# A fused attention and two-layer MLP kernel: the second layer's weights, activations and partial sums handled by other engines, at other times

## The chip, the cores and the metric

One core of one Trainium2 chip runs the whole program. The metric is device microseconds (us) of one execution. Five engines work side by side: TensorE (PE; its weight loads are shown as PEld), VectorE (DVE), ScalarE (ACT), GpSimd (POOL) and SyncE (SP), which here only issues DMAs. Each engine takes its instructions strictly in the order in which they were recorded, so an instruction that waits holds up all that stand behind it on its engine.

## The reference

Inputs are q, k, v (2 batches, 8 heads, 768 tokens, 64 wide, float32) and four weight matrices in float64. An attention with a local window and 24 block summaries gives x (1536 tokens by 512), and two MLP layers follow:

```python
x = attention(q, k, v)                     # 1536 x 512
h = x @ moe_w_in                           # 512 -> 2048
x = (maximum(h, 0) + log1p(exp(-abs(h)))) @ moe_w_out
h = maximum(x @ moe2_w_in, 0)              # second layer
return (h * h) @ moe2_w_out                # 2048 -> 512, float32
```

## The kernel before

Every float32 matrix product is made of three products of rounded parts: each operand is split into a high part (hi, a rounded copy) and a low part (lo, operand minus hi), and TensorE adds hi by hi, hi by lo and lo by hi. So each operand costs a copy and a subtraction on another engine before TensorE may use it.

**First layer** (lines 669 to 730). Weights are held as 16 chunks of 128 hidden columns, in nine slots in SBUF. A step is one chunk by 512 tokens: 12 matmuls into one bank of PSUM (L680), softplus and the hi copy on ScalarE (L686, L687), the lo part on VectorE (L689), and, two steps later, 12 matmuls with the output weights (L706). At the end of a block of tokens the four output banks are added into `part` (L729, VectorE).

**Second layer** (`second`, L792 to L1087). It works in 16 *quads*; a quad is two hidden chunks (f) by one half of the tokens (z, 0 or 1). The first product of a quad is done by Winograd's form of Strassen's scheme, with seven half-size products in place of eight:

- *Activations* (`prepare`, L844 to L890). For each half z, four differences of blocks of `part` (`diff`, L877) and seven splits into hi (L869, ScalarE) and lo (L868, VectorE or GpSimd) give B11, B21, B22, T1 to T4. They are made once per half.
- *Weights* (`w_in`, `w_out`). The float64 words are loaded into one of the `raw` buffers and joined to float32 (`fetch`: L630 on ScalarE, L635 on VectorE, a rescaling copy, L635 again); four sums and differences S1 to S4 (`calc`, L913) and the hi and lo parts (L314/L316 and L927, L940) follow. Of the four raw buffers three (raw0 to raw2) rotate; raw3 holds partial sums.
- *Products* (`quad_in`). `product` is six matmuls of 384 columns (L984) into one of two banks, h0 and h1; here the text calls the seven of a quad p0 to p6. Before, each next product goes to the other bank, and sums of products that Winograd's scheme needs are made in SBUF: `add` (L991, VectorE) adds a bank to a tile `raw3`, `t0` or `t1`.
- *Gates* (`gate`). relu and square (L998), hi (ScalarE), lo (L1001), for each of the four quarters of the hidden block.
- *Outputs* (`quad_out`). Six groups of six matmuls (L1046), here o0 to o5, which work on the gates of the quad before; o0 and o1 go to the two banks of the tile `accp`. When the quads pass to the other half of the tokens, the six banks are first taken out (ACT copy the first time, later L1058 on VectorE: *evacuation*).

TensorE's order within a quad is p0 p1 o0 p2 o1 p3 o2 p4 o3 p5 o4 p6 o5.

**What sets the order.** All work is recorded through `op(engines, costs, due, fn, r, w)` and then laid out by a list scheduler (`Plan.run`, L95): each engine in turn takes, of what is ready by the costs, the operation with the earliest due time; where an operation names two engines, the one that would end first gets it. The due times of the second layer count from T0, the planned end of the first, and from QT per quad. The result is one fixed queue per engine. `rel` holds a load back to 110 us before its due time.

```python
801  quads = [(((q + 1) // 2) % N2, ((q + 2) // 2 + 1) % 2 if q % 2 else (q // 2) % 2) for q in range(2 * N2)]
892  prepare(0, T0 - 20.0)
893  prepare(1, T0 + 8.0)
965  U, V_, C21, E = 3 + q % 2, 0, 1, 2
968  return hb[(q + j) % 2][:, 0:384]
1077 w_in(u, Tq[uses[u][0]])
```

So the quads before are (f, z) = (0,0) (1,0) (1,1) (2,1) (2,0) (3,0) (3,1) ... (7,1) (7,0)... and (0,1) at the end, and each set of weights serves two quads that follow each other, but for the first and the last (nine sets).

Of the kernel before, what the change touches and what calls it, by code (L numbers as in the profile page):

```python
# [8 lines left out]
F32 = mybir.dt.float32  # L9
# [4 lines left out]
ALU = mybir.AluOpType  # L14
# [173 lines left out]
def kernel(  # L188
# [119 lines left out]
    def tt(e):  # L308
        return nc.gpsimd if e == "POOL" else nc.vector
# [304 lines left out]
    def fetch(i, which, wi, wo, f, dl, dv, due):  # L614
# [23 lines left out]
        op(("ACT", "DVE"), (0.75, 0.85), dv, three, w=[RL], rel=due - HOLD)  # L638
        op("DVE", 0.95, dv, lambda: join(ALU.bitwise_and, 0x80000000), r=[RH], w=[RL])
        op(("ACT", "POOL"), (0.67, 0.8), dv, lambda e: copy(e, hi.bitcast(F32), hi.bitcast(F32), 2.0 ** -112), w=[RH])  # L640
        op("DVE", 0.95, dv, lambda: join(ALU.logical_shift_left, 3), r=[RH], w=[RL])
# [150 lines left out]
    def second(T0):  # L792
# [8 lines left out]
        quads = [(((q + 1) // 2) % N2, ((q + 2) // 2 + 1) % 2 if q % 2 else (q // 2) % 2) for q in range(2 * N2)]  # L801
        uses = [[0]] + [[2 * u - 1, 2 * u] for u in range(1, N2)] + [[2 * N2 - 1]]
# [41 lines left out]
        def prepare(z, due):  # L844
# [7 lines left out]
            def split(n, at, due):  # L852
# [39 lines left out]
        prepare(0, T0 - 20.0)  # L892
        prepare(1, T0 + 8.0)
# [8 lines left out]
        def w_in(u, due):  # L902
# [3 lines left out]
            for i, c in ((i0, 2 * f), (i1, 2 * f + 1)):  # L906
                fetch(i, 0, w2_in, w2_out, c, due - 32.0, due - 6.0, due)
# [4 lines left out]
            def calc(to, x, y, o, r, w, d):  # L912
                op(("POOL", "DVE"), (0.8, 0.5), due - 5.0 + d, lambda e: tt(e).tensor_tensor(out=to, in0=x, in1=y, op=o), r=r, w=w)  # L913
# [6 lines left out]
            for j, (x, k_, n) in enumerate(((a, A0, 512), (s12, A1, 512), (s34, B1, 512), (b[:, R_], B0, 256))):  # L920
# [4 lines left out]
                op(("ACT", "POOL"), (0.2 + 0.47 * n / 512, 0.2 + 0.6 * n / 512), d, lambda e, o=o_, j=j, x=x: copy(e, o(j), x),  # L925
                   r=[k_, *key], w=[("wi", u % 2, j, "h")])
                op(("POOL", "DVE"), (0.2 + 1.2 * n / 512, 0.2 + 0.8 * n / 512), d, lambda e, o=o_, j=j, x=x: tt(e).tensor_tensor(  # L927
                    out=o(4 + j), in0=x, in1=o(j).bitcast(F32), op=ALU.subtract), r=[k_, ("wi", u % 2, j, "h"), *key], w=[("wi", u % 2, j, "l")])

        def w_out(v, due):  # L930
            f = quads[uses[v][0]][0]
            for u in range(2):
                i, s = next_raw(), W_OUT[v % 2]
                lo, hi = halves(i)
                fetch(i, 1, w2_in, w2_out, 2 * f + u, due - 32.0, due - 6.0, due)
                o_h, o_l = (ws[s][n] for n in (("ih", "il"), ("oh", "ol"))[u])
# [20 lines left out]
        ng = [0]  # L957
        gat = {}

        def quad_in(q):  # L960
# [33 lines left out]
            def gate(x, f_, blk):  # L994
                i = ng[0] % len(gp)
                ng[0] += 1
                gat[q, f_, blk] = i
                op("DVE", 0.56, URG, lambda: nc.vector.scalar_tensor_tensor(  # L998
                    out=tmp[x], in0=tmp[x], scalar=0.0, in1=tmp[x], op0=ALU.max, op1=ALU.mult), w=[kt(x)])
# [147 lines left out]
    for i, x in enumerate(pend):  # L1147
        finish(x, T + 1.5 + 2 * 2.9 * i, 2.9)
# [42 lines left out]
```

## Time and profile before

| | |
|---|---|
| three runs | 612.46, 613.47 (median), 615.49 us |
| the profiled execution | 614.31 us; span on the core 612.6 us |
| busy, share of the span | PE 590.9 us (96%), DVE 398.9 (65%), POOL 314.8 (51%), ACT 299.8 (49%) |
| granted TensorE clock, mean | 0.988 of full speed |
| chain that ended last, by engine | PE 75%, DVE 14%, DMA 5%, ACT 2% |

"Busy" counts the time from an instruction's start to its end, a wait for a port within it included. The chain is followed back from the last instruction to what released each step. In the lists of groups, "idle" is what an engine waited just before them. Matmuls overlap: six that are listed with 1.21 us follow each other within 1.04 us.

### The profile page before, as it was taken

The numbers are of one execution on the slowest core, as the hardware profiler recorded it, in microseconds if no ns is written. First come the engines' busy times: TensorE is split into PE (matmuls) and PEld (weight loads), VectorE is DVE, ScalarE is ACT, GpSimd is POOL, SyncE is SP. The second block draws the span as 40 slices with busy tenths as digits, with TensorE's granted clock in tenths as the row PEclk, the third lists the DMA queues.
The fourth block names the chain that finished last, engine by engine and source line by source line (L and its number), as shares of the span: only waits on it lengthen the run. The fifth ranks groups of instructions, "written<-read, shape, count | busy, mean of one in ns | idle before, by whom it ended". The sixth has DMA issues, their size and how long they took to land.

```text
span 612.6 us, 9978 instructions
## 1 busy us (share of the span) xinstructions
PE 590.9 (96%) x3905; PEld 517.3 (84%) x3905; DVE 398.9 (65%) x556; ACT 299.8 (49%) x531; POOL 314.8 (51%) x296
## 2 busy tenths in 40 slices
PE   9798999999999999999999997999999999999997
PEld 7677988999888888888888886898888898989996
DVE  5898999726564142652138799876586868687633
ACT  4686888856664144441136363745435343444220
POOL 5877796525650042540018586747565556556421
PEclk9799999999999999999999997999999999999999
DMA  9999622423541032220000420222222222221112
GB/s 283 247 289 224 164 65 56 117 70 109 169 135 35 0 94 80 70 69 1 0 1 1 137 68 1 69 70 70 68 70 68 70 71 69 70 68 35 56 49 103
DMA packets 65871, 53.46 MB, mean 87 GB/s; under 512 B 36384, under 2 KB 59936, under 8 KB 65824
## 3 DMA queue, kind: packets, MB, share of 16 engines
q1 hardware_dynamic: 65824, 52.83, 30.0%
q8 instruction: 30, 0.49, 0.4%
q14 instruction: 17, 0.14, 0.1%
HBM read 49.68 MB, written 3.15 MB: 86 GB/s over the span
## 4 chain that ended last, share of the span: by engine, by line
PE 75%; DVE 14%; DMA 5%; ACT 2%; issue 2%; SPq 1%; POOL 1%; DVEq 0%; ACTq 0%
PE h L680 17%; PE h L984 17%; PE accp L706 10%; PE acc L706 7%; PE acc L1046 7%; PE accp L1046 7%; PE h L1046 7%; DVE raw L635 3%; DMA late<-in_v_dram 2%; DMA raw<-in_moe_w_out_dram 2%; DVE part L877 1%; DVE sm L524 1%; DVE mx L538 1%; DVE s L507 1%; DVE x L868 1%
## 5 line engine op out<-in xcount | busy, mean ns | idle before, releaser
L635 DVE SCALAR_TENSOR_TENSOR raw<-raw 128x512 uint32<-128x512 uint32 x136 | 117.3, 876 | 36.6 <-ACT raw L630 26.7
L680 PE MATMUL h<-x,wih 128*128 128x512 f32 (+1 forms) x480 | 125.4, 349 | 0.0
L680 PEld LDWEIGHTS h<-x,wih 128*128 128x128 f32 x480 | 83.6, 189 | 11.9 <-issue 0.5
L680 PE MATMUL h<-x,wil 128*128 128x512 f32 (+1 forms) x240 | 83.3, 347 | 0.3 <-POOL wil L606 0.3
L686 ACT ACTIVATE h<-h 128x512 f32<-128x512 f32 (+1 forms) x60 | 29.9, 500 | 94.3 <-PE h L680 93.9
L630 ACT ACTIVATE raw<-raw 128x512 uint32<-128x512 uint16 x63 | 42.3, 675 | 39.4 <-DMA raw<-in_moe_w_out_dram 27.8
L680 PEld LDWEIGHTS h<-x,wil 128*128 128x128 f32 x240 | 45.4, 189 | 6.1 <-POOL wil L606 0.5
L984 PE MATMUL h<-x,wil 128*128 128x384 f32 x192 | 39.6, 341 | 2.5 <-ACT woh L314 2.5
L316 POOL TENSOR_SCALAR wih<-raw 128x512 fp32r<-128x512 f32 x17 | 11.6, 683 | 58.4 <-PE h L680 44.8
L314 ACT ACTIVATE raw<-raw 128x512 f32<-128x512 f32 x44 | 29.5, 674 | 21.3 <-DVE raw L635 21.1
L984 PE MATMUL h<-x,wih 128*128 128x384 f32 x192 | 39.3, 340 | 0.3 <-ACT raw L314 0.3
L984 PEld LDWEIGHTS h<-x,wil 128*128 128x128 f32 x192 | 34.8, 192 | 4.2 <-ACT woh L314 2.8
L984 PEld LDWEIGHTS h<-x,wih 128*128 128x128 f32 x192 | 35.0, 192 | 3.2 <-ACT raw L314 0.6
L868 POOL TENSOR_TENSOR x<-part,x 128x768 fp32r<-128x768 f32 x8 | 17.8, 2230 | 37.7 <-ACT x L314 37.7
L316 POOL TENSOR_SCALAR raw<-raw 128x512 f32<-128x512 f32 x24 | 18.2, 765 | 30.1 <-DVE raw L635 27.8
L689 DVE TENSOR_TENSOR g1l<-h,g1h 128x256 fp32r<-128x256 f32 (+1 forms) x24 | 13.2, 549 | 26.2 <-ACT g1h L687 26.2
L984 PE MATMUL h<-x,woh 128*128 128x384 f32 x144 | 29.1, 337 | 0.7 <-DVE t L991 0.7
L913 POOL TENSOR_TENSOR raw<-raw 128x256 f32<-128x256 f32 x25 | 22.6, 906 | 13.7 <-DVE raw L635 6.3
L544 POOL TENSOR_TENSOR s<-s,sm 128x960 f32<-128x960 f32 (+1 forms) x14 | 22.1, 1579 | 13.5 <-DVE sm L526 12.6
L984 PEld LDWEIGHTS h<-x,woh 128*128 128x128 f32 x144 | 25.7, 188 | 3.5 <-DVE t L991 1.5
L991 DVE TENSOR_TENSOR t<-raw,h 128x384 f32<-128x384 f32 x32 | 17.6, 551 | 14.7 <-PE h L984 13.7
L606 POOL TENSOR_TENSOR wol<-raw,woh 128x512 fp32r<-128x512 f32 x14 | 19.8, 1411 | 14.3 <-ACT woh L314 13.9
(349 smaller groups left out, 1588.9 us busy)
## 6 DMA issues: line engine op xcount, KB each, us to landing
raw<-in_moe_w_in_dram SPq DMA_DIRECT2D x34, 512.0 KB, 4.3
raw<-in_moe_w_out_dram SPq DMA_DIRECT2D x34, 512.0 KB, 3.4
vwin<-in_v_dram SPq DMA_DIRECT2D x20, 192.0 KB, 5.3
part<-in_k_dram SPq DMA_DIRECT2D x12, 256.0 KB, 5.0
late<-in_v_dram SPq DMA_DIRECT2D x2, 1536.0 KB, 10.8
out_dram<-part SPq DMA_DIRECT2D x12, 256.0 KB, 2.0
part<-in_q_dram SPq DMA_DIRECT2D x10, 256.0 KB, 5.2
vwin<-in_v_dram SPq DMA_DIRECT2D x4, 160.0 KB, 5.6
```

Of the source, the lines that this page charges most:

```text
L314: nc.scalar.activation(out=out_, in_=in_, func=AF.Copy, **({} if mul is None else {"scale": mul}))
L316: tt(e).tensor_scalar(out=out_, in0=in_, scalar1=1.0 if mul is None else mul, scalar2=1.0, op0=ALU.mult, op1=ALU.mult)
L544: op(("POOL", "DVE"), (1.8 * n + 0.1, 1.75 * n), due, lambda e, sv=sv, rv=rv, spread=spread: tt(e).tensor_tensor(out=sv, in0=sv, in1=sprea ...
L630: nc.scalar.activation(out=lo, in_=q4[:, :, 1], func=AF.Copy, scale=2.0 ** -13, bias=-4095.5 / 8192.0)
L635: nc.vector.scalar_tensor_tensor(out=lo, in0=hi, scalar=n, in1=lo, op0=how, op1=ALU.bitwise_or)
L680: nc.tensor.matmul(out=hview(st), lhsT=ws[s][wn][:, w_], rhs=xx[bl][:, kk, o:o + n], start=(kk == 0 and xx is xh and wn == "ih"), stop=(kk ...
L686: op("ACT", ta, due, lambda: nc.scalar.activation(out=hview(st), in_=hview(st), func=AF.Softplus), w=[H_], tab="sp")
L706: nc.tensor.matmul(out=o, lhsT=a[:, sl], rhs=b, start=(st["first"] and c == 0 and not (A and m % 2)), stop=(st["last"] and c == 2 and not ...
L868: tt(e).tensor_tensor(out=l, in0=i, in1=h.bitcast(F32), op=ALU.subtract)
L913: op(("POOL", "DVE"), (0.8, 0.5), due - 5.0 + d, lambda e: tt(e).tensor_tensor(out=to, in0=x, in1=y, op=o), r=r, w=w)
L984: nc.tensor.matmul(out=bk(b), lhsT=ws[i][m][:, c], rhs=half((z, x, xp), kk), start=first and kk == 0 and n == 0, stop=kk == 1 and n == 2, ...
L1046: nc.tensor.matmul(out=out_bank(j), lhsT=x[:, cs], rhs=y, start=first and u == 0 and n == 0, stop=last and u == 1 and n == 2)
```

## The change

It edits `second` and the little around it:

- **Order of quads:** (0,0) (1,0) (2,0) (2,1) (3,1) (3,0) (4,0) ... (6,1) (7,1) (7,0) (0,1) (1,1). The first three quads work on half 0, so half 1 is wanted at the fourth quad and no more at the third; the last two need chunk pairs 0 and 1 again, which makes ten sets of weights (two more loads of each matrix).
- **Due times:** the activations of half 0 are due at T0 - 27 (before: T0 - 20), of half 1 at T0 + 24 (before: T0 + 8); the first two sets of weights at T0 - 80 and T0 - 45 (w_in), T0 - 75 and T0 - 40 (w_out).
- **Products:** even steps of Winograd's sum stay in bank h0, and TensorE adds the next product onto them; ScalarE copies the sum out between (`keep`). h1 takes p1, p3, p6. Three `add` are left of five. The quarter C21 is squared straight from the bank.
- **Engines:** `diff`, the lo parts of the activations and of the gates go to VectorE alone; `calc` and the lo parts of the weights to GpSimd alone; their hi parts and the two conversions of `fetch` to ScalarE alone.
- The last steps of the first layer are given slightly more planned time (3.6 for 2.9).

```diff
-        quads = [(((q + 1) // 2) % N2, ((q + 2) // 2 + 1) % 2 if q % 2 else (q // 2) % 2) for q in range(2 * N2)]
-        uses = [[0]] + [[2 * u - 1, 2 * u] for u in range(1, N2)] + [[2 * N2 - 1]]
+        quads, uses = [(0, 0), (1, 0), (2, 0)], []
+        while len(quads) < 2 * N2 - 2:
+            f, z = quads[-1]
+            quads += [(f, 1 - z), (f + 1, 1 - z)] if f + 1 < N2 else [(f, 1 - z)]
+        quads += [(0, 1), (1, 1)]
...
-                op(("POOL", "DVE"), (2.0, 1.0), due, lo, r=[K[at], ("x2", z, n, "h")] + lk[z, n, "l"], w=[("x2", z, n, "l")])
+                op("DVE", 0.9, due, lambda: lo("DVE"), r=[K[at], ("x2", z, n, "h")] + lk[z, n, "l"], w=[("x2", z, n, "l")])
...
-        prepare(0, T0 - 20.0)
-        prepare(1, T0 + 8.0)
+        prepare(0, T0 - 27.0)
+        prepare(1, T0 + 24.0)
...
-                op(("POOL", "DVE"), (0.8, 0.5), due - 5.0 + d, lambda e: tt(e).tensor_tensor(out=to, in0=x, in1=y, op=o), r=r, w=w)
+                op("POOL", 0.85, due - 5.0 + d, lambda: nc.gpsimd.tensor_tensor(out=to, in0=x, in1=y, op=o), r=r, w=w)
...
-            U, V_, C21, E = 3 + q % 2, 0, 1, 2
+            U, V_, C21, U2 = 0, 1, 2, 3 + q % 2
 
             def bk(j):
-                return hb[(q + j) % 2][:, 0:384]
+                return hb[j][:, 0:384]
...
-                op(("POOL", "DVE"), (1.1, 0.56), URG, lambda e: tt(e).tensor_tensor(
+                op("DVE", 0.56, URG, lambda: nc.vector.tensor_tensor(
                     out=gview2(i)[1], in0=tmp[x], in1=gview2(i)[0].bitcast(F32), op=ALU.subtract),
...
+            def keep(x, b):
+                op("ACT", 0.5, URG, lambda: copy("ACT", tmp[x], bk(b)), r=[kb_(b), *r3], w=[kt(x)])
             product(0, "A11", "B11", 0, True)
-            op("ACT", 0.5, URG, lambda: copy("ACT", tmp[U], bk(0)), r=[kb_(0), *r3], w=[kt(U)])
-            product(1, "S2", "T2", 1, True)
+            keep(U, 0)
+            product(1, "A12", "B21", 1, True)
             add(U, U, 1)
-            product(2, "A12", "B21", 0, False)
-            op("ACT", 0.5, URG, lambda: nc.scalar.activation(out=tmp[E], in_=bk(0), func=AF.Relu), r=[kb_(0), *r3], w=[kt(E)])
-            gate(E, 0, 0)
-            product(3, "S3", "T3", 1, True)
-            add(V_, U, 1)
-            product(4, "S1", "T1", 0, True)
-            product(5, "A22", "T4", 1, False)
-            add(C21, U, 1)
-            gate(C21, 1, 0)
+            gate(U, 0, 0)
+            product(2, "S2", "T2", 0, False)
+            keep(U2, 0)
+            product(3, "S1", "T1", 1, True)
+            product(4, "S3", "T3", 0, False)
+            keep(V_, 0)
+            add(V_, V_, 1)
+            gate(V_, 1, 1)
+            product(5, "A22", "T4", 0, False)
             yield
-            add(V_, V_, 0)
-            gate(V_, 1, 1)
-            product(6, "S4", "B22", 0, False)
-            add(U, U, 0)
-            gate(U, 0, 1)
+            gate(C21, 1, 0, 0)
+            product(6, "S4", "B22", 1, False)
+            add(U2, U2, 1)
+            gate(U2, 0, 1)
...
-            w_in(u, Tq[uses[u][0]])
-            w_out(u, Tq[uses[u][0] + 1])
+            w_in(u, T0 - (80.0, 45.0)[u])
+            w_out(u, T0 - (75.0, 40.0)[u])
```

What it moves, at three places. In all of them raw_74 to raw_77 are raw0 to raw3, t_1818 and t_1819 are t0 and t1, h_107 and h_108 are h0 and h1, x tiles hold the split activations, and tiles named wih, wil, woh, wol with a number are parts of the weight slots.

*GpSimd's queue across the passage from the first layer to the second*, before:

```order
L868 TENSOR_TENSOR x_73<-part,x_73 128x768
L877 TENSOR_TENSOR part<-part 128x2x384 x2
L868 TENSOR_TENSOR x_73<-part,x_73 128x768 x2
L868 TENSOR_TENSOR x_1817<-part,x_1817 128x768
L316 TENSOR_SCALAR wil_87<-raw_75 128x512
L927 TENSOR_TENSOR wih_90<-raw_75,wih_86 128x512
L927 TENSOR_TENSOR woh_92<-raw_76,woh_88 128x512
L940 TENSOR_TENSOR wil_95<-raw_74,wih_94 128x512
```

and of the change:

```order
L935 TENSOR_TENSOR wih_90<-raw_75,wih_86 128x512
L935 TENSOR_TENSOR wil_91<-raw_75,wil_87 128x512
L935 TENSOR_TENSOR woh_92<-raw_76,woh_88 128x512
L935 TENSOR_TENSOR wol_93<-raw_76,wol_89 128x256
L948 TENSOR_TENSOR wil_95<-raw_74,wih_94 128x512
L948 TENSOR_TENSOR wol_97<-raw_75,woh_96 128x512
```

The four subtractions and two differences of activations are gone from this queue; all lo parts of the second set of weights stand on it, four of which VectorE shared before.

*VectorE's queue after the last evacuation of the middle block of the first layer* (L729 into `part`), of the change; L689 is the lo part of a first-layer step, L885 is `diff` and L876 the lo part of an activation:

```order
L729 TENSOR_TENSOR part<-acc_1821,part 128x512
L885 TENSOR_TENSOR part<-part 128x2x384 x2
L876 TENSOR_TENSOR x_1817<-part,x_1817 128x768
L876 TENSOR_TENSOR x_73<-part,x_73 128x768
L885 TENSOR_TENSOR part<-part 128x2x384
L876 TENSOR_TENSOR x_73<-part,x_73 128x768
L885 TENSOR_TENSOR part<-part 128x2x384
L876 TENSOR_TENSOR x_73<-part,x_73 128x768
L689 TENSOR_TENSOR g1l<-h_107,g1h 128x512
```

Before, one difference and one subtraction of half 0 stood ahead of that L689 on VectorE, one of each behind it, and the rest on GpSimd; now all eight stand between that L729 and the L689.

*ScalarE's queue in one quad of the steady stretch*, before (L1010 takes p2 out of its bank):

```order
L314 ACTIVATE raw_77<-h_107 128x384
L1010 ACTIVATE edge<-h_107 128x384
L314 ACTIVATE woh_1805<-edge 128x384
L630 ACTIVATE raw_74<-raw_74 128x512
L630 ACTIVATE raw_76<-raw_76 128x512
L314 ACTIVATE raw_76<-raw_76 128x512
L314 ACTIVATE g0h<-t_1818 128x384
```

and of the change, from the copy of p0 (t_1818<-h_107) to the one that frees h0 for p5 (t_1819<-h_107):

```order
L314 ACTIVATE t_1818<-h_107 128x384
L314 ACTIVATE woh_84<-raw_74 128x512
L314 ACTIVATE wih_86<-raw_75 128x512
L314 ACTIVATE woh_1805<-t_1818 128x384
L314 ACTIVATE raw_77<-h_107 128x384
L630 ACTIVATE raw_76<-raw_76 128x512
L314 ACTIVATE raw_76<-raw_76 128x512
L630 ACTIVATE raw_74<-raw_74 128x512
L314 ACTIVATE t_1819<-h_107 128x384
```

Where ScalarE read a bank twice early in a quad, it now reads one four times, and the third of these stands behind two conversions (L630) that wait for a DMA and a rescaling copy that waits for VectorE.

## Rows read from the trace of the kernel before

**Rows 1.** Busy time by stretch: the passage between the layers, the steady stretch; columns named.
```profile
core 0: us, PE busy (x) PEld busy (x) DVE busy (x) ACT busy (x) POOL busy (x), PEclk, DMA share, GB/s
343.00:386.00 43.00, 37.67 (x172) 32.74 (x171) 42.40 (x48) 22.32 (x42) 33.43 (x24) 0.92 0.16 49
395.54:600.72 205.18, 203.97 (x1015) 182.70 (x1015) 142.16 (x208) 81.18 (x147) 113.13 (x105) 1.00 0.19 62
```
**Rows 2.** Waits of PE, 319 to 381 us, then 381 to 601 us: total, times, longest.
```profile
PE h L984 <- ACT woh L314: 2.5, 1, 2.5
PE h L984 <- DVE t L991: 2.5, 2, 1.8
...
PE accp L1046 <- DVE part L1058: 1.2, 2, 0.6
```
**Rows 3.** Timeline of PE from the second layer's first product: start, duration, [idle before].
```profile
341.83 1.23 PE L984 MATMUL h<-x,wih 128*128 128x384 f32 x6
...
367.99 1.62 PE L984 MATMUL h<-x,wol 128*128 128x384 f32 x6 [1.77 <-DVE t L991]
369.41 0.63 PE L1046 MATMUL h<-wih,wih 128*128 128x512 f32 x1
369.83 0.63 PE L1046 MATMUL h<-wil,wih 128*128 128x512 f32 x1
...
379.18 2.26 PE L984 MATMUL h<-x,wil 128*128 128x384 f32 x6 [2.52 <-ACT woh L314]
```
**Rows 4.** The chain of waits: start, duration, what; the fourth and fifth quad, then the end.
```profile
395.54 2.08 PE h L984 x12
397.62 1.39 PE accp L1046 x6
...
411.18 2.08 PE h L984 x12
...
600.72 2.73 PE accp L1046 x12
```
**Rows 5.** Timeline of VectorE in the passage, then of GpSimd.
```profile
361.82 2.60 DVE L877 TENSOR_TENSOR part<-part 128x768 f32<-128x768 f32 x1
...
364.81 2.20 DVE L868 TENSOR_TENSOR wih<-part,woh 128x384 fp32r<-128x384 f32 x1
...
364.50 2.09 POOL L877 TENSOR_TENSOR part<-part 128x768 f32<-128x768 f32 x1 [0.90 <-DVE part L877]
```
**Rows 6.** Single lines, whole run: duration ns min/median/max, first and last start.
```profile
L991 DVE TENSOR_TENSOR raw<-raw,h x32: 536/542/555, 347.0 to 599.4; 128x384 f32<-128x384 f32 x32
...
L998 DVE SCALAR_TENSOR_TENSOR t<-t x32: 546/558/2165, 352.0 to 597.6; 128x384 f32<-128x384 f32 x32
...
L868 DVE TENSOR_TENSOR x<-part,x x4: 946/2036/2637, 309.2 to 369.8; 128x768 fp32r<-128x768 f32 x4
...
L635 DVE SCALAR_TENSOR_TENSOR raw<-raw x136: 642/694/2282, 13.0 to 566.7; 128x512 uint32<-128x512 uint32 x136
...
L1001 POOL TENSOR_TENSOR wol<-t,woh x10: 1010/1020/1452, 379.2 to 580.8; 128x384 fp32r<-128x384 f32 x10
...
L940 POOL TENSOR_TENSOR wil<-raw,wih x9: 1311/1331/1738, 260.4 to 570.1; 128x512 fp32r<-128x512 f32 x9
```
**Rows 7.** Timeline, one quad of the steady stretch: p2 on PE, its reader on ACT.
```profile
509.29 1.21 PE L984 MATMUL h<-x,wih 128*128 128x384 f32 x6
...
510.60 0.49 ACT L1010 ACTIVATE edge<-h 128x384 f32<-128x384 f32 x1 [2.85 <-PE h L984]
```
**Rows 8.** Timeline of ACT: second conversion of a quad, two late ones.
```profile
469.58 0.67 ACT L630 ACTIVATE raw<-raw 128x512 uint32<-128x512 uint16 x1 [0.25 <-DMA raw<-in_moe_w_in_dram]
...
514.49 0.68 ACT L630 ACTIVATE raw<-raw 128x512 uint32<-128x512 uint16 x1 [0.83 <-DMA raw<-in_moe_w_in_dram]
```
**Rows 9.** Timeline around o1 of a quad that evacuates: DVE, then PE.
```profile
478.20 0.68 DVE L1058 TENSOR_TENSOR part<-accp,part 128x512 f32<-128x512 f32 x1
...
478.93 0.50 PE L1046 MATMUL accp<-wih,woh 128*128 128x512 f32 x1 [0.63 <-DVE part L1058]
```

More of the change, by code (lines that the diff above doesn't have):

```diff
@@ L612, in halves, with fetch @@
         return r[:, :, 0], r[:, :, 1]
-    def fetch(i, which, wi, wo, f, dl, dv, due):
+    def fetch(i, which, wi, wo, f, dl, dv, due, own=False):
         lo, hi = halves(i)
@@ L637, in fetch @@
         op("SP", 0.6, dl, load, w=[RL, RH], kb=348, rel=due - HOLD - 10.0)
[L638 to L641, printed above, removed]
+        op(*(("ACT", 0.67) if own else (("ACT", "DVE"), (0.75, 0.85))), dv, (lambda: three("ACT")) if own else three, w=[RL], rel=due - HOLD)
+        op("DVE", 0.75 if own else 0.95, dv, lambda: join(ALU.bitwise_and, 0x80000000), r=[RH], w=[RL])
+        op(*(("ACT", 0.67) if own else (("ACT", "POOL"), (0.67, 0.8))), dv, lambda e="ACT": copy(e, hi.bitcast(F32), hi.bitcast(F32), 2.0 ** -112), w=[RH])
+        op("DVE", 0.75 if own else 0.95, dv, lambda: join(ALU.logical_shift_left, 3), r=[RH], w=[RL])
     g_t, tmp = [], []
@@ L800, in second @@
         N2 = NF // 2
-        quads = [(((q + 1) // 2) % N2, ((q + 2) // 2 + 1) % 2 if q % 2 else (q // 2) % 2) for q in range(2 * N2)]
-        uses = [[0]] + [[2 * u - 1, 2 * u] for u in range(1, N2)] + [[2 * N2 - 1]]
+        quads, uses = [(0, 0), (1, 0), (2, 0)], []
[3 more added lines that the diff above has]
+        quads += [(0, 1), (1, 1)]
+        for q, (f, z) in enumerate(quads):
+            if q and quads[q - 1][0] == f:
+                uses[-1].append(q)
+            else:
+                uses.append([q])
         use_of = {q: u for u, x in enumerate(uses) for q in x}
@@ L876, in flat @@
                     return v if S[n][0] == 3 or 3 not in bs else v.rearrange("p k (b t) -> p k b t", b=3)
-                op(("DVE", "POOL"), (1.0, 2.0), due, lambda e: tt(e).tensor_tensor(
+                op("DVE", 0.9, due, lambda: nc.vector.tensor_tensor(
                     out=flat(to), in0=flat(a), in1=flat(b_), op=ALU.subtract),
@@ L934, in w_out @@
                 lo, hi = halves(i)
-                fetch(i, 1, w2_in, w2_out, 2 * f + u, due - 32.0, due - 6.0, due)
+                fetch(i, 1, w2_in, w2_out, 2 * f + u, due - 32.0, due - 6.0, due, True)
                 o_h, o_l = (ws[s][n] for n in (("ih", "il"), ("oh", "ol"))[u])
                 k_ = ("raw", i, 0)
-                op(("ACT", "POOL"), (0.67, 0.8), due - 4.0, lambda e, o_h=o_h, lo=lo: copy(e, o_h, lo.bitcast(F32)),
+                op("ACT", 0.67, due - 4.0, lambda o_h=o_h, lo=lo: copy("ACT", o_h, lo.bitcast(F32)),
                    r=[k_, ("slot", s)], w=[("wo", v % 2, u, "h")])
-                op(("POOL", "DVE"), (1.4, 1.0), due - 4.0, lambda e, o_h=o_h, o_l=o_l, lo=lo: tt(e).tensor_tensor(
+                op("POOL", 1.4, due - 4.0, lambda o_h=o_h, o_l=o_l, lo=lo: nc.gpsimd.tensor_tensor(
                     out=o_l, in0=lo.bitcast(F32), in1=o_h.bitcast(F32), op=ALU.subtract),
@@ L956, in out_bank @@
             return acc[j] if j < 4 else hb[j - 2]
-        ng = [0]
+        gfree = list(range(len(gp)))
         gat = {}
@@ L992, in add, with gate, square @@
                    r=[kb_(b)] + ([kt(x)] if x != to else []), w=[kt(to)])
[L994 to L996 removed]
+            def gate(x, f_, blk, psum=None):
+                i = gfree.pop(0)
                 gat[q, f_, blk] = i
[L998 to L999 removed]
+                def square():
+                    if psum is None:
+                        nc.vector.scalar_tensor_tensor(out=tmp[x], in0=tmp[x], scalar=0.0, in1=tmp[x], op0=ALU.max, op1=ALU.mult)
+                    else:
+                        nc.vector.tensor_tensor(out=tmp[x], in0=bk(psum), in1=tmp[x], op=ALU.mult)
+                if psum is not None:
+                    op("ACT", 0.5, URG, lambda: nc.scalar.activation(out=tmp[x], in_=bk(psum), func=AF.Relu),
+                       r=[kb_(psum), *r3], w=[kt(x)])
+                op("DVE", 0.56, URG, square, r=[] if psum is None else [kb_(psum)], w=[kt(x)])
                 op("ACT", 0.52, URG, lambda: copy("ACT", gview2(i)[0], tmp[x]), r=[kt(x), gp[i]], w=[("gg", i, "h")])
[L1001 removed]
+                op("DVE", 0.56, URG, lambda: nc.vector.tensor_tensor(
                     out=gview2(i)[1], in0=tmp[x], in1=gview2(i)[0].bitcast(F32), op=ALU.subtract),
@@ L1061, in quad_out @@
                     op("SP", 0.5, due, lambda t=t, pt=pt: nc.sync.dma_start(out=out[128 * t:128 * t + 128, :], in_=pt), r=[kp], kb=256)
+            gfree.extend(gat[q, u, blk] for u in range(2) for blk in sorted({j // 3 for j in js}))
             if last and 5 in js:
@@ L1147 @@
     for i, x in enumerate(pend):
[L1148 removed]
+        finish(x, T + 2.0 + 2 * 3.6 * i, 3.6)
     second(T)
```

8 lines of the change are left out of this document (4 added, 4 removed).

## Prediction

> **What bounds the kernel now.** I read busy time by stretch first [rows 1]. In the steady stretch of the second layer, 395.54 to 600.72 us, PE is busy 203.97 of 205.18 us at full clock, and VectorE, ScalarE and GpSimd have 63, 124 and 92 us to spare. In the passage from the first layer to the second, 343 to 386 us, it is the other way round: PE 37.67 of 43 at a clock of 0.92, VectorE 42.40 of 43, GpSimd 33.43. So time can be won in the passage, and elsewhere there is little to win.
>
> How much? The chain [rows 4] gives the price of a quad: the fourth begins at 395.54, the fifth at 411.18, so 15.64 us, made of seven products of 1.04 (two in 2.08) and six output groups of 1.39. Thirteen quads fill 395.54 to 600.72: 13 x 15.64 = 203.3, so 1.9 us are lost there. From the first product at 341.83 [rows 3] to 395.54 there are 53.71 us. What PE has to do in it is three quads, without outputs for the first (6 x 1.39 = 8.34 less), and the last 24 matmuls of the first layer (four groups' worth, 5.56): 46.92 - 8.34 + 5.56 = 44.14. So 9.6 us are lost in the passage, **11.4 us in all**, and a change that leaves the matmuls alone can win no more.
>
> Where the 9.6 go: PE's waits [rows 2] hold a wait of 2.5 for a hi copy on ScalarE and 2.5 for two adds on VectorE, and a little more; the two long ones stand in PE's timeline at 367.99 and 379.18 [rows 3]. That is some 5.3 with short ones. The rest is the clock: behind the first of these waits matmuls of 512 columns start 0.42 apart (369.41, 369.83), against 1.39 / 6 = 0.23 in the steady stretch. The granted clock falls after PE has waited, to the lower of its levels, so each wait is paid nearly twice.
>
> Why VectorE is late shows in its rows [rows 5, 6]. L991, with one input in PSUM, takes 536 to 555 ns at all times. L998, L868 and L635, with both inputs in SBUF, take 546, 946 and 642 at best and 2165, 2637 and 2282 at worst. At 364.81 a subtraction of 128x384 takes 2.20 on VectorE, under a difference that runs on GpSimd from 364.50 for 2.09 [rows 5]. So in the passage the two engines hold each other up; 42.40 busy is mostly waiting for the other's reads.
>
> **The change, part by part.**
>
> *Engines.* An operation that moves from GpSimd to VectorE gets cheaper: L1001 takes 1.01 to 1.02 on GpSimd [rows 6], and its like on VectorE (L998, same size) 0.55; L868 takes 0.95 alone. What the changed queues issue between the passage's first and last add, at undisturbed prices: on VectorE with two inputs in SBUF 7 joins (0.69), 7 squares and 12 subtractions of 384 (0.55), 5 subtractions and 4 differences of 768 (0.95) = 4.8 + 10.5 + 8.6 = 23.9. Those that read PSUM are 9 at 0.55 and 4 evacuations at 0.69, 7.7. Sum 31.6 where 42.4 stood. GpSimd keeps 12 operations; all at the dearest, L940's 1.33, they take 16.0 against 33.4. If no operation with two SBUF inputs runs beside GpSimd at all, the pair needs 23.9 + 16.0 = 39.9 of the 43 us. It fits, with some 3 us spare and the queue's order still to be met. So I take 1.5 us of the 9.6 as staying; at the least 0, at the most 5 (the two longest waits once each with its clock).
>
> The Trainium skill ("Perfetto Trace Analysis", section "Optimizing Scalar/DVE Operations") warns that GpSimd and VectorE share a read port of SBUF, so that work moved between the two might not help. That would speak against this part, and by it the sum would stay near 612, the first rival below. The rows agree that the two hold each other up (2.20 for 0.55), but they show also that the same work holds the port half as long on VectorE.
>
> *Activations of half 0 earlier.* Eight operations of some 0.95, 7.6 us, now stand on VectorE between the last evacuation of a block and an L689. The L706 that needs that L689 comes two steps later, and a step is 24 matmuls of 0.23, so 11 us away. PE's work covers it: 0. If they stretched to L868's median of 2.04, 16.3, it would be 5 us; GpSimd has only weights then, so I stay near 0.
>
> *First weights earlier.* The first lo part of a weight runs at 260.4 [rows 6] in L940, 80 us before it is needed; the first set was ready before. Worth 0; that the second set is ready sooner counts in the passage.
>
> *Partial sums in one bank.* Two of five adds go, copies go to ScalarE (81.18 us over 13 quads [rows 1], 6.2 of 15.6 per quad; now some 8.6). No bound, but order counts. h0 is used again after one output group: from the start of p2 or p4 to the next product in the bank there are 1.04 + 1.39 = 2.43 us. Its reader starts 1.31 after the product and takes 0.49 [rows 7], so 0.6 us are spare: 0 where ScalarE is free. Where it isn't, PE waits. The copy ahead of p5 stands behind two conversions L630, which wait for DMAs. p5 is due 5 x 1.04 + 4 x 1.39 = 10.8 into the quad, so the second L630 (0.68) must start by 10.8 - 0.5 - 0.7 = 9.6. At 514.49 [rows 8] it started 8.6 into its quad (p2 stands 3.4 in and began at 509.29 [rows 7]); at 469.58 [rows 8], 11.5 into a quad that began near 395.54 + 4 x 15.64 = 458.1. A start like the former costs nothing, one like the latter 1.9 us. I take 0.5 for all steady quads together, and at most 4 (two such quads).
>
> *Evacuation.* o1 waits for VectorE to empty the bank of o0: PE idles 0.63 at 478.93, and 1.2 us in two quads [rows 2, 9]. The copies of 0.68 are unchanged, but GpSimd's lo of the output weights now always runs there. I expect some 0.5 in four quads, 2.0; at least 0, at most 3 by the long form of [rows 9] with its clock.
>
> *Ten sets of weights for nine.* Two more loads of each matrix; the DMA share is 0.19 [rows 1], so hidden.
>
> **Sum.** The profiled execution took 614.31. 614.31 - 11.4 + 1.5 (passage) + 0.5 + 2.0 (steady) = 606.9. The median of the runs is 0.84 below the profiled one: **606.1 us**. With nothing lost it would be 602.1; with 5 and 7 lost, 614.1.
>
> **Rivals.** 0.5% (about what a measurement of this kernel can tell from no change) is 3.1 us: 610.4 and 616.5 are the bounds.
>
> *The passage stays bound by VectorE.* The conversions, gates and activations of half 1 all meet there still, VectorE alone has all the subtractions, and one that is late drags PE's clock down. For it: the spare 3 of 43 us; against it, that half 1 is wanted one quad later and GpSimd's load halves. If 7 of the 9.6 stay, with the steady 2.5: 614.31 - 11.4 + 7 + 2.5 - 0.84 = 611.6; this case spreads over 609 to 614.
>
> *The copy ahead of p5 is late in every quad* (slower). ScalarE's queue is fixed, and a load that lands late holds the L630s, the copy and so p5, with the clock after it. If two thirds of 13 quads are 1.9 late, 16.5 us are added: 622.6. It decides as soon as the wait reaches (613.5 - 606.1) / 13 = 0.57 per quad, which is an L630 that starts later than 10.2 into every quad. For it: [rows 8], 469.58. Against it: loads of one queue that come earlier by their due times, and the early one at 514.49.
>
> *The change does less than it says*, the scheduler having undone it: the orders above show that it doesn't; no chance of its own.
>
> **How the numbers follow.** Forecast (602 to 610.4) 0.62, and 0.04 for a time about or below 602; passage still bound 0.22, a fifth of it still below 610.4; late copies 0.12. So faster 0.71, same 0.17, slower 0.12. The range 602.0 to 613.0 leaves out the 0.04, the 0.12 and the last fifth of the passage's case, 0.2 in all. The likeliest case's own range is 602 to 610.4.
>
> **What would show it.** Right: PE waits under 2 us in all between 343 and 396, a granted clock of 0.97 or more in 343 to 386, VectorE busy 32 to 37 and GpSimd under 18 there, quads of 15.64 us after it. Wrong: waits of PE's product line for ScalarE's copy out of h at p5, or an L630 later than 9.6 in its quad (late copies); VectorE above 40 of 43 again, with two-input operations of over 1.5 us (passage bound); PE idle at o1 for the evacuation by more than 3 us in all. The prediction is wrong if the wait for the add of p0 + p1 has only become a wait for a copy.

## The result, and the profile after it

The changed kernel takes **606.92 us** (median of four runs, 605.77 to 607.26), the kernel before 614.09 in the same comparison: a ratio of 0.9881, 95% interval 0.9851 to 0.9910. The forecast was 606.1.

| | before | after |
|---|---|---|
| the profiled execution, us | 614.31 | 607.07 |
| its span | 612.6 | 605.4 |
| busy PE / DVE / POOL / ACT, us | 590.9 / 398.9 / 314.8 / 299.8 | 586.3 / 396.6 / 247.6 / 330.9 |
| granted TensorE clock, mean | 0.988 | 0.997 |

In the code after the change the lines are shifted: L992 is the product (L984 before), L999 `add`, L1008 the square, L1010 the square from the bank, L1016 the lo part of a gate, L876 and L885 `split` and `diff`, L1063 the outputs, L1075 the evacuation, L921, L935 and L948 the weights.

Busy time by stretch, after (compare [rows 1]):

```profile
core 0: us, PE busy (x) PEld busy (x) DVE busy (x) ACT busy (x) POOL busy (x), PEclk, DMA share, GB/s
343.00:386.00 43.00, 43.00 (x218) 38.82 (x217) 35.98 (x60) 28.31 (x53) 16.79 (x14) 1.00 0.19 62
395.54:600.72 205.18, 204.29 (x1007) 181.32 (x1006) 150.74 (x225) 104.01 (x197) 74.66 (x62) 1.00 0.23 72
```

In the passage PE has no gap left, 43.00 of 43 at full clock where it had 37.67 at 0.92. VectorE does more operations (60 for 48) in less busy time (35.98 for 42.40), GpSimd is at half.

The chain of waits after, the same places as in [rows 4], and the first product:

```profile
343.32 2.10 PE h L992 x12
...
387.58 2.08 PE h L992 x12
...
403.22 2.08 PE h L992 x12
...
593.45 2.73 PE accp L1063 x12
```

The fourth quad begins 44.26 us after the first product; 44.14 is the least that the matmuls allow. Before, the two starts were 53.55 us apart. The prediction's 53.71 took the first product from the timeline (341.83) and the fourth quad from the chain (395.54), and the chain gives these starts 0.16 later than the timeline does. In PE's timeline the fourth quad before and the first product after are:

```profile
395.38 1.20 PE L984 MATMUL h<-x,wih 128*128 128x384 f32 x6
```
```profile
343.16 2.27 PE L992 MATMUL h<-x,wih 128*128 128x384 f32 x12
```

A quad is 15.64 as it was. Thirteen of them take 593.45 - 387.58 = 205.87, which is 2.55 over 13 x 15.64 (before 1.86). So of the 7.24 us between the two profiled executions 9.29 come out of the passage, 0.7 go back in the steady stretch, and 1.33 are lost ahead of it: in the timeline the first product starts at 343.16 and not at 341.83. That start moves by itself: in four of the traces below, whose attention and first layer are the same, it lies at 341.65 (twice), 341.88 and 342.50, the last in another execution of the unaltered change.

What PE's weight loads wait for from 343 to 601 us, after (total, times, longest):

```profile
PEld accp L1063 <- DVE part L1075: 2.2, 5, 0.5
PEld h L992 <- ACT t L314: 0.7, 1, 0.7
PEld accp L1063 <- DVE g2l L1016: 0.3, 1, 0.3
```

The wait of o1 for the evacuation [rows 2, 9] has stayed and comes five times; one wait for a copy out of h0 is new. The wait for a hi part and those for adds are gone.

Single lines of VectorE after 345 us (ns min/median/max), against [rows 6]:

```profile
L1008 DVE SCALAR_TENSOR_TENSOR t<-t x32: 543/559/1646, 346.6 to 588.4; 128x384 f32<-128x384 f32 x32
...
L876 DVE TENSOR_TENSOR x<-part,x x5: 944/949/949, 361.7 to 371.5; 128x768 fp32r<-128x768 f32 x5
...
L885 DVE TENSOR_TENSOR part<-part x4: 946/948/952, 363.1 to 374.6; 128x768 f32<-128x768 f32 x4
```

Activations of half 1 now take their lone price of 0.95 every time; before, the one like them took up to 2.64. Squares still stretch: to 1.65 in this line, and one on another tile to 1.67 within the passage (at 356.13). Counted in the trace, 19 of the 40 squares after 386 us take more than 0.6, and GpSimd is at work during each of these 19.

How the two engines meet, after. GpSimd first, then VectorE (start, duration):

```profile
372.37 2.24 POOL L948 TENSOR_TENSOR wil<-raw,wih 128x512 fp32r<-128x512 f32 x1 [14.98 <-ACT wih L314]
...
384.74 0.86 POOL L921 TENSOR_TENSOR raw<-raw 128x256 f32<-128x256 f32 x1
385.55 1.18 POOL L921 TENSOR_TENSOR raw<-raw,raw 128x256 f32<-128x256 f32 x1
```
```profile
371.55 0.95 DVE L876 TENSOR_TENSOR x<-part,x 128x768 fp32r<-128x768 f32 x1
372.42 0.55 DVE L1016 TENSOR_TENSOR g0l<-edge,g0h 128x384 fp32r<-128x384 f32 x1
372.88 0.55 DVE L1008 SCALAR_TENSOR_TENSOR raw<-raw 128x384 f32<-128x384 f32 x1
...
384.79 1.22 DVE L1016 TENSOR_TENSOR g1l<-t,g1h 128x384 fp32r<-128x384 f32 x1
```

Here it goes both ways. At 372.37 VectorE keeps its 0.55 twice and GpSimd's lo part takes 2.24 for 1.31; at 384.79 VectorE pays, 1.22 for 0.55. The Trainium skill ("SBUF — State Buffer", section "Who interferes with whom") says that which of the two was issued first decides who is blocked. The second place agrees: GpSimd's operation at 384.74 began first. The first agrees only in part: VectorE's subtraction of 371.55 was running when GpSimd's began, but the two operations of VectorE behind it began after GpSimd's and were not held up either.

### The profile page after: what moved, and what is told of

It reads as the page before. It is cut to its first block, busy times and chain, and to the rows that moved or that the text cites. A ratio compares the mean times of both kernels' runs of the same rounds, so it can differ in the third digit from the quotient of the medians.

```text
span 605.4 us, 9947 instructions
## 1 busy us (share of the span) xinstructions
PE 586.3 (97%) x3905; PEld 512.6 (85%) x3905; DVE 396.6 (66%) x581; ACT 330.9 (55%) x599; POOL 247.6 (41%) x235
## 4 chain that ended last, share of the span: by engine, by line
PE 76%; DVE 12%; DMA 5%; ACT 2%; POOL 1%; issue 1%; SPq 1%; ACTq 0%; POOLq 0%
PE h L680 19%; PE h L992 16%; PE accp L706 12%; PE acc L706 8%; PE h L1063 7%; PE acc L1063 7%; PE accp L1063 6%; DMA raw<-in_moe_w_in_dram 3%; DVE raw L635 2%; DMA vwin<-in_v_dram 2%; DVE sm L524 1%; DVE mx L538 1%; DVE s L507 1%; SPq L390 1%; PE ab L569 1%
## 5 line engine op out<-in xcount | busy, mean ns | idle before, releaser
L630 ACT ACTIVATE raw<-raw 128x512 uint32<-128x512 uint16 x67 | 44.8, 671 | 18.4 <-DMA raw<-in_moe_w_in_dram 9.4
L948 POOL TENSOR_TENSOR wil<-raw,wih 128x512 fp32r<-128x512 f32 x10 | 14.6, 1457 | 87.8 <-ACT wih L314 72.0
L314 ACT ACTIVATE raw<-raw 128x512 f32<-128x512 f32 x57 | 38.2, 672 | 17.9 <-DVE raw L635 17.9
L935 POOL TENSOR_TENSOR wih<-raw,wih 128x512 fp32r<-128x512 f32 x10 | 14.9, 1489 | 77.1 <-ACT wih L314 77.1
L921 POOL TENSOR_TENSOR raw<-raw 128x256 f32<-128x256 f32 x30 | 28.3, 945 | 29.6 <-DVE raw L635 29.1
L992 PE MATMUL h<-x,wil 128*128 128x384 f32 x192 | 38.5, 336 | 0.0
L992 PEld LDWEIGHTS h<-x,wil 128*128 128x128 f32 x192 | 34.4, 188 | 2.7
L992 PE MATMUL h<-x,wih 128*128 128x384 f32 x192 | 35.9, 335 | 0.0
L992 PEld LDWEIGHTS h<-x,wih 128*128 128x128 f32 x192 | 33.8, 188 | 1.4
L689 DVE TENSOR_TENSOR g1l<-h,g1h 128x256 fp32r<-128x256 f32 (+1 forms) x24 | 13.2, 550 | 26.3 <-ACT g1h L687 26.2
L314 ACT ACTIVATE woh<-raw 128x512 fp32r<-128x512 f32 (+1 forms) x34 | 22.2, 654 | 14.1 <-DVE raw L1008 6.0
L999 DVE TENSOR_TENSOR t<-t,h 128x384 f32<-128x384 f32 x32 | 17.6, 550 | 18.0 <-ACT t L314 12.3
L992 PE MATMUL h<-x,woh 128*128 128x384 f32 x144 | 28.9, 335 | 0.0
L316 POOL TENSOR_SCALAR wih<-raw 128x512 fp32r<-128x512 f32 x10 | 7.4, 736 | 52.5 <-PE h L680 44.8
L314 ACT ACTIVATE t<-h 128x384 f32<-128x384 f32 x32 | 15.6, 487 | 21.8 <-PE h L992 21.8
```

Source lines behind the costliest of these rows:

```text
L314: nc.scalar.activation(out=out_, in_=in_, func=AF.Copy, **({} if mul is None else {"scale": mul}))
L630: nc.scalar.activation(out=lo, in_=q4[:, :, 1], func=AF.Copy, scale=2.0 ** -13, bias=-4095.5 / 8192.0)
L921: op("POOL", 0.85, due - 5.0 + d, lambda: nc.gpsimd.tensor_tensor(out=to, in0=x, in1=y, op=o), r=r, w=w)
L935: op("POOL", 0.2 + 1.2 * n / 512, d, lambda o=o_, j=j, x=x: nc.gpsimd.tensor_tensor(out=o(4 + j), in0=x, in1=o(j).bitcast(F32), op=ALU.sub ...
L992: nc.tensor.matmul(out=bk(b), lhsT=ws[i][m][:, c], rhs=half((z, x, xp), kk), start=first and kk == 0 and n == 0, stop=kk == 1 and n == 2, ...
L999: op("DVE", 0.58, URG, lambda: nc.vector.tensor_tensor(out=tmp[to], in0=tmp[x], in1=bk(b), op=ALU.add), r=[kb_(b)] + ([kt(x)] if x != to e ...
```

## The experiments

Three theories were set against each other. **P**, of the prediction: VectorE and GpSimd hold each other up, and the new assignment of engines is the gain. **Q**: the order of the quads is. **S**: the sums in one bank are.

| kernel | median, us | ratio to before, 95% |
|---|---|---|
| the change | 606.92 | 0.9881 (0.9851 to 0.9910) |
| the change again | 606.03 | 0.9873 (0.9856 to 0.9889) |
| engines undone | 616.79 | 1.0035 (1.0020 to 1.0050) |
| quads undone | 606.87 | 0.9880 (0.9852 to 0.9907) |
| sums undone | 605.82 | 0.9859 (0.9831 to 0.9887) |
| due times undone | 608.04 | 0.9898 (0.9869 to 0.9927) |
| before, activations and gates alone | 608.40 | 0.9903 (0.9876 to 0.9929) |
| before, weights alone | 616.95 | 1.0050 (1.0035 to 1.0065) |
| change, no GpSimd | 604.04 | 0.9836 (0.9813 to 0.9859) |
| before, no GpSimd | 603.68 | 0.9833 (0.9818 to 0.9849) |
| copy ahead of p5 three times | 614.12 | 0.9996 (0.9981 to 1.0011) |
| outputs reordered, three groups left out | 601.07 | 0.9783 (0.9768 to 0.9797) |
| outputs reordered, whole | 604.72 | 0.9851 (0.9831 to 0.9871) |

### One part undone

Engines:

```diff
-                op("DVE", 0.9, due, lambda: lo("DVE"), ...
+                op(("POOL", "DVE"), (2.0, 1.0), due, lo, ...
...
-                op("POOL", 0.85, due - 5.0 + d, ...
+                op(("POOL", "DVE"), (0.8, 0.5), due - 5.0 + d, ...
```

> The changed kernel, but each operation may again go to either of its two engines, with the planned costs of before (differences, lo parts, calc, hi parts, the conversions of fetch). Theory P (VectorE and GpSimd hold each other up; putting the activations and gates on VectorE alone and weights on GpSimd alone is what freed the passage): 610 to 614 us, GpSimd again over 25 us busy in 343 to 386, two-input operations of VectorE over 1.5 us there, PE waits of 3 us or more. Rival Q (the order of the quads alone did it, by giving half 1 a quad more time) and rival S (the sums in one bank did it): 606 to 608, with no wait of PE in the passage.

It takes 616.79 us, above the 610 to 614 that P expected and 2 to 5 thousandths over the kernel before: all of the gain is gone, and a little more. By stretch, then PE's gaps in its timeline, then a pair of GpSimd and VectorE:

```profile
343.00:386.00 43.00, 37.50 (x173) 32.47 (x172) 39.63 (x41) 23.83 (x44) 34.38 (x25) 0.92 0.19 62
```
```profile
358.35 1.32 PE L992 MATMUL h<-x,wil 128*128 128x384 f32 x6 [1.71 <-ACT t L314]
370.92 1.82 PE L992 MATMUL h<-x,wol 128*128 128x384 f32 x6 [2.23 <-ACT t L314]
374.30 2.29 PE L992 MATMUL h<-x,woh 128*128 128x384 f32 x6 [1.56 <-DVE t L999]
```
```profile
361.30 1.46 POOL L876 TENSOR_TENSOR wih<-part,woh 128x384 fp32r<-128x384 f32 x1
...
361.81 1.36 DVE L1008 SCALAR_TENSOR_TENSOR t<-t 128x384 f32<-128x384 f32 x1
```

The passage looks as it did before the change, with one difference: PE now waits for ScalarE's copies out of h0 (1.71, 2.23), because these stand behind work that waits for VectorE (on ScalarE 1.53 for a square ahead of the first, 2.01 for a join ahead of the second). So P. That the sums in one bank are the weaker form when VectorE is late, and so the little more, is a reading of these two waits; no run separates it.

Quads:

```diff
-        quads, uses = [(0, 0), (1, 0), (2, 0)], []
...
+        quads = [(((q + 1) // 2) % N2, ((q + 2) // 2 + 1) % 2 if q % 2 else (q // 2) % 2) for q in range(2 * N2)]
...
-        prepare(1, T0 + 24.0)
+        prepare(1, T0 + 8.0)
```

> The changed kernel with the old order of the quads, (0,0) (1,0) (1,1) ..., so that half 1 is wanted at the third quad, and its activations due at T0 + 8 as before. P: half of the loss comes back, 609 to 612, VectorE near its limit (over 38 of 43 us in 343 to 386). Q: nearly all of it, 612 to 616. S: 606 to 608.

```profile
343.00:386.00 43.00, 42.90 (x215) 38.22 (x214) 36.66 (x59) 30.20 (x57) 15.77 (x15) 1.00 0.19 62
```

No loss: 606.87, and PE all but full in the passage (42.90) though half 1 is wanted a quad earlier. Q falls, and with it my own expectation that half of the gain hung on the order.

Sums (the lines of `quad_in` from before):

> The changed kernel with the old sums: five adds into SBUF on VectorE and banks h0 and h1 in turn. P: two more operations of 0.55 us per quad on VectorE, which has room for them: 606.5 to 609. S (PE waited for adds because the chain from product to product went through them): 611 to 615, PE waiting for L999's add again. Q: 606 to 608.

605.82 us, a little below what P expected and no slower than the change; the intervals overlap. VectorE is busy 39.31 of 43 in the passage, with PE still without a gap. S falls.

Due times (T0 - 20 for half 0, the quads' own for the first weights, 2.9 for the last steps):

> The changed kernel with the old due times: half 0 at T0 - 20, the first two sets of weights at their quads, the last steps of the first layer planned at 2.9 each. P: the first set was ready in the first layer anyhow, so 606 to 608.5; at most one wait of PE for half 0 or for the second set, under 2 us. A rival that has the readiness within the first layer as the cause: 610 or more, with PE waiting within the first two quads.

608.04 us; its interval overlaps that of the change. PE has one wait, of 0.6 us, for a copy out of h0, and none for a weight or for half 0: the first weights were indeed ready before.

### One part alone

```diff
-                op(("POOL", "DVE"), (2.0, 1.0), due, lo, ...
+                op("DVE", 0.9, due, lambda: lo("DVE"), ...
-                op(("DVE", "POOL"), (1.0, 2.0), due, lambda e: tt(e).tensor_tensor(
+                op("DVE", 0.9, due, lambda: nc.vector.tensor_tensor(
-                op(("POOL", "DVE"), (1.1, 0.56), URG, lambda e: tt(e).tensor_tensor(
+                op("DVE", 0.56, URG, lambda: nc.vector.tensor_tensor(
```

> The kernel before with one part of the change alone: differences and lo parts of the activations and lo parts of the gates on VectorE only; weights as before on either engine. If the stretched pairs in the passage are what cost (theory P), this is most of the gain, since it takes some 17 us of GpSimd's 33 in 343 to 386 away: 605.5 to 609 us, PE waits under 2 us in the passage, clock 0.97 or more there. If the weights were what crowded VectorE (rival W): 611 to 615.

```profile
343.00:386.00 43.00, 42.42 (x214) 38.12 (x214) 37.66 (x59) 22.76 (x42) 12.62 (x11) 1.00 0.15 50
```
```profile
PE accp L1046 <- DVE part L1058: 2.2, 2, 1.1
```

Three lines changed give 608.40 us: the passage is all but free (42.42 of 43), and what is left is mostly o1's wait for the evacuation, here 2.2 us in two quads.

The other engines, weights alone (`calc` and lo parts on GpSimd, hi parts and conversions on ScalarE):

> The kernel before with the other part of the engines alone: calc and lo parts of the weights on GpSimd only, their hi parts and conversions on ScalarE only; activations and gates on either as before. P: GpSimd keeps its long operations with two inputs in SBUF and gets more: 611 to 617, VectorE still over 40 of 43 us in the passage. W: 605.5 to 609.

By stretch, then GpSimd, then VectorE:

```profile
343.00:386.00 43.00, 36.05 (x167) 30.68 (x167) 37.16 (x43) 22.26 (x41) 31.16 (x23) 0.96 0.15 46
```
```profile
372.27 2.10 POOL L868 TENSOR_TENSOR x<-part,x 128x768 fp32r<-128x768 f32 x1 [1.77 <-ACT x L314]
```
```profile
372.58 2.21 DVE L998 SCALAR_TENSOR_TENSOR t<-t 128x384 f32<-128x384 f32 x1
```

616.95 us, slower than before. P had the time right, but not VectorE's busy time, which it put over 40. VectorE's sum of work (37.16 of 43) does not explain the loss; single operations do: a square of 0.55 takes 2.21 under a subtraction of 768 columns on GpSimd, and a product waits for the add that follows it. Such waits of PE for adds come to 7.0 us between 343 and 396.

### GpSimd taken out

```diff
-                op("POOL", 0.85, due - 5.0 + d, lambda: nc.gpsimd.tensor_tensor(
+                op("DVE", 0.5, due - 5.0 + d, lambda: nc.vector.tensor_tensor(
...
-                op("POOL", 1.4, due - 4.0, lambda ...: nc.gpsimd.tensor_tensor(
+                op("DVE", 0.7, due - 4.0, lambda ...: nc.vector.tensor_tensor(
```

> The changed kernel with calc and the lo parts of the second layer's weights on VectorE too, so that GpSimd does nothing in the second layer. P (it is GpSimd's work that stretches VectorE's operations with two SBUF inputs): after 345 us L1008 and L1016 take 0.54 to 0.57 without exception, L876 of 768 columns 0.95, L635 0.69; VectorE does 11 operations more per quad but loses the stretch, so 604 to 610 us, and the waits of o1 for the evacuation get shorter or go if the stretch made them. Rival (VectorE stretches by its own queue or by ScalarE and the DMAs): operations over 1 us remain.

Busy time by stretch, then the steady stretch of the changed kernel beside it, then single lines of VectorE after 345 us:

```profile
343.00:386.00 43.00, 43.00 (x218) 38.77 (x217) 37.11 (x66) 24.86 (x48) 0.00 (x0) 1.00 0.19 61
395.54:590.00 194.46, 194.46 (x968) 174.09 (x967) 150.61 (x282) 103.30 (x199) 0.00 (x0) 1.00 0.23 74
```
```profile
395.54:590.00 194.46, 193.57 (x959) 172.30 (x958) 144.75 (x215) 102.74 (x195) 74.66 (x62) 1.00 0.23 72
```
```profile
L1008 DVE SCALAR_TENSOR_TENSOR t<-t x32: 548/550/559, 345.1 to 584.7; 128x384 f32<-128x384 f32 x32
```

No square takes over 0.56 any more, joins 0.68 to 0.70. From 395.54 to 590 PE has no gap at all. VectorE does 282 operations there in 150.61 us of busy time, the changed kernel 215 in 144.75: the 67 more cost it 5.9 us, since nothing stretches. The wait of o1 for the evacuation, 2.2 us in five quads of the change, is down to 0.3, once. The time is 604.04 us. Its interval (0.9813 to 0.9859) overlaps that of the change (0.9851 to 0.9910) a little, so the times of this kernel alone do not show that it is faster; the next one's do.

The same on the old order, old due times and old sums:

> The kernel before with the engines alone changed, and further than the change does it: in the second layer everything that stood on either VectorE or GpSimd on VectorE, hi parts and conversions on ScalarE; old order of quads, old due times, old sums in two banks. P (GpSimd beside VectorE was the whole cost): 603 to 607 us, as fast as the changed kernel or faster, no PE wait over 1 us in the passage. If order, due times or sums are needed too: 608 to 612.

```profile
343.00:386.00 43.00, 43.00 (x218) 38.89 (x217) 36.98 (x68) 21.80 (x41) 0.00 (x0) 1.00 0.11 37
395.54:590.00 194.46, 194.46 (x971) 174.63 (x970) 158.74 (x300) 87.91 (x162) 0.00 (x0) 1.00 0.20 65
```

603.68 us, where the change on the same chip took 606.03; the intervals (to 0.9849, from 0.9856) do not touch. So neither the order of the quads, nor the due times, nor the sums are needed for the gain, and this version beats both kernels. Since these three showed no effect of their own beyond the intervals, the difference is put down to GpSimd: what the change left on it cost more than it carried.

### The copy ahead of p5

```diff
             keep(V_, 0)
+            keep(V_, 0)
+            keep(V_, 0)
```

> The changed kernel with the copy of p4 out of h0 (ahead of p5) made three times, the same values each time: about 1.0 us more on ScalarE between p4 and p5. By the bounds of the prediction 0.6 us are spare, so p5 waits 0.4 or more in each of 16 quads, with some clock after it: 612 to 618 us. If the spare time is larger (the reader overlaps with the product's end, or the products' order gives more), under 608.5 and no wait of p5 in most quads.

614.12 us, within what was expected, but not in the place expected. PE's timeline, p5 and p6 of one quad and p0 and p1 of the next:

```profile
450.73 1.31 PE L992 MATMUL h<-x,wol 128*128 128x384 f32 x6
451.88 1.20 PE L992 MATMUL h<-x,woh 128*128 128x384 f32 x6
455.76 3.47 PE L992 MATMUL h<-x,wih 128*128 128x384 f32 x12 [2.68 <-DVE edge L1010]
```

The planner knows of the two copies more and here puts all output groups ahead of p5; then p0 waits 2.68 for the square of C21 out of h0, while copies out of h0 hold PE's weight loads for 0.9 in two places only. So this run shows what the two copies cost together with the order that the planner then chose, some 7 us over the change. What p5 alone would bear, and whether 0.6 us are spare, it does not show.

### The order of the outputs

```diff
-            for j in js:
+            for at, j in zip(js, [0, 2, 1, 3, 4, 5][js[0]:js[-1] + 1]):
...
-                due = T_ + QT / 7 * (j + 1.5)
+                due = T_ + QT / 7 * (at + 1.5)
```

The wait of o1 in the changed kernel, VectorE and then PE's loads, in the timeline:

```profile
452.41 1.31 POOL L948 TENSOR_TENSOR wol<-raw,woh 128x512 fp32r<-128x512 f32 x1 [0.86 <-ACT woh L314]
...
452.92 1.21 DVE L1008 SCALAR_TENSOR_TENSOR t<-t 128x384 f32<-128x384 f32 x1
...
454.06 0.68 DVE L1075 TENSOR_TENSOR part<-accp,part 128x512 f32<-128x512 f32 x1
...
454.79 0.19 PEld L1063 LDWEIGHTS accp<-wih,wih 128*128 128x128 f32 x1 [0.45 <-DVE part L1075]
```

A square stretched by GpSimd's lo part (1.21 for 0.55) delays the evacuation of o0 by about as much as PE then waits, although o1 writes the other bank of the tile `accp`.

> The changed kernel unaltered, as the yardstick for the three beside it on the same chip: 605.8 to 607.5 us, o1 waiting for the evacuation some 0.4 us in five quads.

> The changed kernel with the first three output groups of a quad in the order o0, o2, o1, so that the two banks of the tile accp are no longer written in turn with one product between. Theory T (o1 waits because it writes the other half of the tile that VectorE is emptying): its five waits, 2.5 us of PE time, go, 604.0 to 605.3 us. Rival U (VectorE is late there in any case, and whatever group follows waits): no gain, 606 to 607.5, the waits moved to o2 or to the next group on accp.

This first form left out the groups o3 to o5 of the last quad and what comes of them; with three groups of 1.36 it would take, by estimate, 601.07 + 4.1 = 605.2. Its steady stretch has PE at 194.46 of 194.46, which is T. The whole form:

> The changed kernel with the output groups in the order o0, o2, o1, o3, o4, o5 in every quad, and all six in the last one. T: the five waits of o1 for the evacuation are gone as in the run before it, where the steady stretch held PE without a gap, so 1.5 to 2.5 us less than the changed kernel on the same footing: 603.7 to 605.3 us. U: 605.8 to 607.5, with the waits moved to another group.

```profile
395.54:590.00 194.46, 194.46 (x971) 174.77 (x970) 146.73 (x218) 103.82 (x197) 74.88 (x62) 1.00 0.22 72
```

No wait for L1075 is left in its trace, and from first product to the last outputs there are 590.94 - 343.10 = 247.84 us, against 592.22 - 342.50 = 249.72 in the change run again, which was on another chip. So o1 waited for the tile, not for its bank, and the gap is worth 1.9 us by the traces. In the measured times it is 604.72 to 606.03, with intervals that overlap: not shown there.

## Why the prediction was right

Point by point, in its own steps.

- **What bounds the kernel** held: the passage was the place, and its loss was the gain. That loss was 9.4 us (9.6 in the prediction, by the mixed views), and 9.3 came back. The term "1.5 stays" was too careful, 0.1 did. The port sum that it came from (39.9 of 43 us) was right in its outcome, not in its making. It counts 48 operations on VectorE from the first add to the last, which lie at 345.53 and 381.88, so in 37 us and not in 43; ten joins stand there and not seven, and in the 43 us there are 60 operations. Against this, the records overlap where one operation follows another (at 372.42 and 372.88 two of 0.55 start 0.46 apart), so a sum of recorded times is too long. That the outcome (VectorE 35.98 for 31.6, GpSimd 16.79 for 16.0) still fitted is in part two errors against each other, which is luck.
- **Engines**: right, and stronger than I put it. Undone, they cost the whole gain (616.79); alone, in their half for activations and gates, they bring most of it (608.40). The rule of the Trainium skill ("Perfetto Trace Analysis", section "Optimizing Scalar/DVE Operations") that was weighed there is that moving work between these two might not help. Here it did not decide: VectorE needs half the time for the same operation (0.55 for 1.01), so the move took time out of the shared reads. It agrees with the move the other way, weights to GpSimd with their hi parts on ScalarE, which alone is slower than before.
- **Activations and first weights earlier**: 0, as said. No PE wait stands at the end of the first layer, and with the old dates 608.04 is not clear of 606.92.
- **Partial sums**: the 0.5 us had one instance, the wait of 0.26 (0.7 at the weight load) at 477.24. But the bound of 9.6 us for the second L630 was wrong. ScalarE's timeline there, then PE's p5:

```profile
474.64 0.68 ACT L630 ACTIVATE raw<-raw 128x512 uint32<-128x512 uint16 x1 [2.96 <-DMA raw<-in_moe_w_in_dram]
475.22 0.67 ACT L314 ACTIVATE raw<-raw 128x512 f32<-128x512 f32 x1
476.13 0.68 ACT L314 ACTIVATE raw<-raw 128x512 f32<-128x512 f32 x1 [0.25 <-DVE raw L635]
476.71 0.47 ACT L314 ACTIVATE t<-h 128x384 f32<-128x384 f32 x1
```
```profile
477.24 0.45 PE L992 MATMUL h<-x,wol 128*128 128x384 f32 x1 [0.26 <-ACT t L314]
```

  This L630 starts 8.6 us into its quad (466.04, the next after 449.98), a whole microsecond earlier than my bound, and p5 still waits: two rescaling copies, one of which waits for a join on VectorE, stand between it and the copy. I had counted the L630 alone. The rival built on it, late in every quad, did not come: this is the one late copy of the run.
- **Evacuation**: 2.0 in four quads was put down; 2.2 in five came.
- **Not in the sum**: the start of the second layer, 1.33 later in this execution. It hides that the passage gave back 1.2 more than forecast; without either the profiled time would have been about the same 607. So part of the closeness is luck.
- **The rival of the bound passage** was argued with half 1's quad order as help. The order was no help: undone, it costs nothing. The order and the ten sets of weights have no effect on the time beyond the intervals, some 0.3%.

What stays open: whether the sums in one bank cost some 1 us (605.82 without them) and whether the later due times cost as much (608.04); both lie within the intervals. Nor does any run separate the activations from the gates, or the two ways in which GpSimd cost time: its own operations, twice as long, and the stretch that they put on VectorE's.

## What to carry to other kernels

Where VectorE and GpSimd both work on operands in SBUF, read the max beside the median of VectorE's two-input lines: a median of 0.56 with a max of 2.17 meant here that the second engine held the first one up. Price an operation on both engines before sharing it; if GpSimd needs twice the time and the first engine has a third of its span to spare, as here, try it with GpSimd left out. And where one engine empties one bank of a tile while another fills its neighbour, look for a wait: here a group of other work between the two removed it; a tile for each bank was not tried.

## What was not expected

That GpSimd was worth less than nothing: I had taken its half load as the fit, not as the rest of the cost. Without it 67 more operations on VectorE in 194 us cost only 5.9 us of its time, and PE lost nothing by it. And that weights alone on GpSimd, with VectorE at 37.16 of 43, was slower than before: a single operation stretched from 0.55 to 2.21 in a chain counts, not the sum of the busy time.
